# A gated FFN behind windowed attention: a hand-ordered start, a shorter lag between attention and FFN, and another order of loads

## The chip, the cores and the metric

The kernel runs on one core of one Trainium2 chip. The metric is the device time of one execution in microseconds (us); lower is better. A kernel is timed several times, and I quote the median with the lowest and highest run. Runs are sorted into fast and slow (for this one-core kernel a run is slow when it lies over 1.5% above the fastest run of the same kernel). The reported time is about 1.7 us longer than the span of the profile (234.69 against 233.0 us for the profiled run of the kernel before).

## The reference

Eight sequences of 576 positions go through attention with 8 heads of 64. Four heads see a window of 32 positions, four see every fourth position of a window of 128. Then one of eight experts is picked **per sequence**, from the mean over the whole sequence, and applied to all of it.

```python
# attention (cut): scores masked to window 32, or to window 128 with step 4; softmax; attn @ v -> x (8, 576, 512)
pooled = x.mean(axis=1)
logits = pooled @ w_gate
e_idx = np.argmax(logits, axis=1)              # one expert for a whole sequence
...
h = np.maximum(x[mask] @ w1[e], 0.0)           # w1[e]: 512 x 1024
out[mask] = gate_w[mask, None, None] * (h @ w2[e])
```

What matters is a dependence: no weight of a sequence's FFN can be fetched before **all** of its attention is done, because the address of w1 and w2 is the gate's result. In between must be other work, or the TensorE (PE) waits.

## The kernel before

Attention is cut into slots, four to a batch (one slot is two heads). The FFN of batch b runs in four slots too: two for the first matmul (FFN1, with w1), two for the second (FFN2, with w2, and a tail of 64 rows). `LAGS` says how many slots after its attention a batch's FFN runs. Batch 0 has 7, so that the pipeline starts early, the others have 8, so that slot 11 has no FFN work.

```python
LAGS = (7, 8, 8, 8, 8, 8, 8, 8)
...
for b in range(B):
    for kk in range(NSLOT):                        # NSLOT = 4
        runs[NSLOT * b + kk + LAGS[b]] = (b, kk)   # slot t runs quarter kk of the FFN of batch b
...
for t in range(max(runs) + 1):
    ...                                            # items: quarter of an FFN in this slot
    pa(); fence()                                  # first half of attention x V of slot t-1
    flush()                                        # issues the output stores of the last FFN2 slot
    emit_S_mm(b, n); emit_exp(b, n)                # scores of slot t
    run_T(t)                                       # transposes of q or k for a later slot
    ...
    for i, f in enumerate(items[:k0]):             # first half of this slot's FFN work
        f()
        if i == k0 // 2 and gn == 0 and 1 < gb < B + 1:
            emit_gate(gb - 1)                      # gate of batch b: in slot 4b + 5
    ...
    emit_norm(pb, pn)                              # normalise slot t-1; after a batch's last: its mean
    for i, f in enumerate(items[k0:]):             # second half of the FFN work
        f()
```

The gate reads the index into a register of GpSimd (POOL), which then issues the loads. They all go through one software queue (q0 on the page), in this order:

```python
def emit_gate(b):
    ...                                            # four small matmuls, argmax, index to a register
    for a in range(2):
        for g in range(2):                         # w1[e] in four requests, float32 in memory, bf16 in the tile
            nc.gpsimd.dma_start(out=w1b[...], in_=moe_w1[ds(e_val, 1), ...])
    if b == 0:
        load_va(2); load_qb(2)
    load_vb(b + 2)
    nc.gpsimd.dma_start(out=w2b[:], in_=moe_w2[ds(e_val, 1)]...)
    load_qa(b + 3); load_va(b + 3); load_qb(b + 3) # q, k and v, up to three batches ahead
```

Output rows are stored by SyncE (SP) through another queue (q1 on the page). The first seven slots, before any FFN work, were emitted by the same loop in a fixed order.

The softmax here doesn't subtract the row's maximum and nothing guards it: scores larger than these inputs give would overflow.

## Time and profile before

| | before |
|---|---|
| time, median of 3 runs | 232.99 us (232.79 to 236.41) |
| span of the profile | 233.0 us |
| PE busy | 85% |
| mean granted PE clock | 0.967 |
| gate of batch 0, first FFN matmul | 30.15, 41.88 us |
| gate to gate, batches 1 to 7, mean | 24.1 us |

The next lines are from the page of the kernel before: the PE's busy time; then busy tenths of PE, granted PE clock and DMA in 40 slices of the span; then the chain that ended last, by engine and by line.

```profile
PE 199.2 (85%) x3938; PEld 138.9 (60%) x3952; DVE 128.6 (55%) x368; ACT 129.1 (55%) x231; POOL 80.6 (35%) x128
...
PE   0577665999952999999999799999999999999992
...
PEclk9999999999985599999999999999999999999998
DMA  5999319999999947999999999999996299489823
...
PE 74%; DMA 8%; issue 6%; ACT 4%; DVE 4%; POOL 2%; POOLq 1%; SPq 0%
```

After the start the PE is nearly full. The exception is near 66 to 81 us, with the slot that has no FFN work, an idle of 4.5 us that the profile calls "issue" (the engine waited for nothing that the profile shows), and a half clock (granted 0.50 from 67.63 to 81.28). The DMA engines are busy nearly throughout: the packets of the software queue take 90.3% of sixteen engines' span, those of the store queue 12.2%.

How a batch gets its weights in time is seen in one batch. The next lines are from the timeline of PE in the kernel before, batch 3 (start, duration, engine, line, operation, tiles, count). L476 is the gate, L534 is FFN1, L554 and L569 are FFN2 and its tail. (x15 stands where 16 ran: this trace lacks 14 records of L554, x242 in place of x256. A row at the end of a window is cut off there.)

```profile
108.39 0.34 PE L476 MATMUL m<-wg_t,pooled 128*1 128x8 f32 x8
109.24 2.61 PE L534 MATMUL m<-xt,w1b 128*128 128x288 bf16 x20 [0.51 <-DVE mx L481]
...
113.45 3.63 PE L554 MATMUL m<-w2b,ht 128*128 128x512 bf16 x15
...
118.62 3.63 PE L554 MATMUL m<-w2b,ht 128*128 128x512 bf16 x15
122.18 1.06 PE L569 MATMUL m<-w2b,ht 128*64 128x256 bf16 x16
...
124.76 1.52 PE L534 MATMUL m<-xt,w1b 128*128 128x288 bf16 x11
```

And the timelines of POOL and of SP for the same stretch, the first line being w1's requests, the second the first stores of batch 2:

```profile
110.78 2.40 POOL L490 DMA_DIRECT2D w1b<-in_moe_w_dram  x4 [10.39 <-DVE ht L541]
...
117.92 0.81 SPq L562 DMA_DIRECT2D out_dram<-osb  x2
```

The gate runs at 108.39 and w1 is first used at 124.76, that is 16.4 us later, all of it filled: half a slot of FFN1, both slots of FFN2 of the batch before, and attention. The w1 requests go out at 110.78, and the trace has their last landing at 120.78, 4 us before the use.

In the tail there is no attention left to fill with. Batch 7 in the timeline of PE of the kernel before:

```profile
200.53 0.35 PE L476 MATMUL m<-wg_t,pooled 128*1 128x8 f32 x8
...
203.67 7.08 PE L554 MATMUL m<-w2b,ht 128*128 128x512 bf16 x31
210.68 1.06 PE L569 MATMUL m<-w2b,ht 128*64 128x256 bf16 x16
211.68 0.42 PE L534 MATMUL m<-xt,w1b 128*128 128x288 bf16 x2
212.47 7.75 PE L534 MATMUL m<-xt,w1b 128*128 128x288 bf16 x62 [0.37 <-DMA w1b<-in_moe_w_dram]
```

Here w1 and its use just meet: the wait is 0.37 us.

### The profile page before, as it was taken

Reading aid. Unit: us, or ns where it says so; the run is one execution under the profiler, and the core shown is the slowest. Engines: PE = TensorE matmul, PEld = TensorE weight load, DVE = VectorE, ACT = ScalarE, POOL = GpSimd, SP = SyncE. Lnnn points to the kernel's source line nnn. Section 1 sums busy time; section 2 is a strip of 40 time slices with the busy share of each in tenths; the row PEclk is TensorE's granted clock in tenths of the full one; section 3 lists DMA queues with packets and bytes.
Section 4 is the critical chain, followed back from the end, with each engine's and each line's share of the span. In section 5 each row is a group of like instructions: output and inputs, shape, how many; then the busy total and the mean of one; then the engine's idle time right before and its main releaser. Section 6 shows DMA issues by size and latency. Waiting matters only on the chain.

```text
span 233.0 us, 9018 instructions
## 1 busy us (share of the span) xinstructions
PE 199.2 (85%) x3938; PEld 138.9 (60%) x3952; DVE 128.6 (55%) x368; ACT 129.1 (55%) x231; POOL 80.6 (35%) x128
## 2 busy tenths in 40 slices
PE   0577665999952999999999799999999999999992
PEld 0556455775651676587658565777577746746741
DVE  2765464665652465686558466667566657415312
ACT  2466755676552377666865566577657763431420
POOL 7873037640934009520862048405500400130000
PEclk9999999999985599999999999999999999999998
DMA  5999319999999947999999999999996299489823
GB/s 86 180 191 192 72 29 163 190 205 204 178 225 230 204 89 114 160 254 237 207 210 234 239 150 167 205 254 206 199 242 177 44 160 230 137 139 247 177 93 113
DMA packets 49383, 40.97 MB, mean 176 GB/s; under 512 B 23744, under 2 KB 37056, under 8 KB 49344
## 3 DMA queue, kind: packets, MB, share of 16 engines
q0 software_dynamic: 42880, 30.94, 90.3%
q1 hardware_dynamic: 6464, 9.46, 12.2%
q8 instruction: 31, 0.51, 0.8%
q14 instruction: 8, 0.07, 0.1%
HBM read 61.88 MB, written 9.44 MB: 306 GB/s over the span
## 4 chain that ended last, share of the span: by engine, by line
PE 74%; DMA 8%; issue 6%; ACT 4%; DVE 4%; POOL 2%; POOLq 1%; SPq 0%
PE m L534 28%; PE m L554 21%; PE nd L323 8%; DMA w1b<-in_moe_w_dram 6%; PE m L243 5%; PE ps L264 3%; PE m L569 3%; DMA km<-in_k_dram 3%; PE e L323 2%; ACT pt L288 1%; DVE qk L253 1%; ACT qk L251 1%; DVE pt L295 1%; PE m L521 1%; ACT lnd L420 1%
## 5 line engine op out<-in xcount | busy, mean ns | idle before, releaser
L534 PE MATMUL m<-xt,w1b 128*128 128x288 bf16 x512 | 70.5, 296 | 3.0 <-issue 1.6
L534 PEld LDWEIGHTS <-w1b 128*128 128x128 bf16 x512 | 49.9, 101 | 18.8 <-issue 4.1
L554 PE MATMUL m<-w2b,ht 128*128 128x512 bf16 x242 | 56.9, 380 | 1.0 <-issue 0.2
L490 POOL DMA_DIRECT2D w1b<-in_moe_w_dram x32 | 19.1, 612 | 103.5 <-PE m L534 55.9
L539 ACT ACTIVATE ht<-m 128x288 bf16<-128x288 f32 x64 | 26.3, 411 | 30.1 <-PE m L534 26.5
L288 ACT ACTIVATE pt<-ps 128x896 bf16<-128x896 f32 x32 | 29.2, 912 | 23.3 <-PE ps L264 23.3
L554 PEld LDWEIGHTS <-ht 128*128 128x128 bf16 x256 | 23.8, 98 | 27.7 <-DMA w2b<-in_moe_w_dram 0.2
L541 DVE TENSOR_SCALAR ht<-m 128x288 bf16<-128x288 f32 x64 | 28.2, 453 | 13.9 <-PE m L534 13.0
L453 DVE SCALAR_TENSOR_TENSOR xt<-nd,rd 128x320 bf16<-128x320 f32 (+1 forms) x52 | 26.0, 537 | 11.9 <-ACT rd L426 11.9
L253 DVE COPY qk<-m 128x576 bf16<-128x576 bf16 x23 | 17.4, 756 | 22.6 <-PE m L243 22.4
L323 PEld LDWEIGHTS <-vm 64*64 64x64 bf16 x896 | 17.6, 116 | 19.1 <-issue 13.1
L295 DVE TENSOR_TENSOR pt<-pt,mk 128x896 bf16<-128x896 bf16 x32 | 19.8, 620 | 11.5 <-ACT pt L288 11.4
L121 POOL DMA_DIRECT2D vm<-in_v_dram x32 | 24.3, 783 | 5.3 <-DMA qm<-in_q_dram 2.4
L323 PE MATMUL nd<-pt,vm 64*64 64x64 bf16 (+1 forms) x736 | 18.7, 195 | 5.1 <-DMA w1b<-in_moe_w_dram 2.6
L426 ACT ACTIVATE rd<-lnd 128x576 f32<-128x576 f32 x32 | 21.9, 683 | 0.9
L323 PE MATMUL nd<-pt,ones 64*64 64x256 bf16 (+2 forms) x236 | 17.0, 247 | 4.5 <-issue 4.5
L420 ACT ACTIVATE lnd<-nd 128x576 f32<-128x576 f32 x26 | 16.7, 642 | 7.3 <-PE nd L323 7.3
L561 DVE TENSOR_SCALAR osb<-m,gbc 128x512 f32<-128x512 f32 x16 | 12.0, 750 | 15.6 <-PE m L554 15.5
L243 PEld LDWEIGHTS <-km 64*64 64x64 bf16 x576 | 14.7, 123 | 7.9 <-DMA km<-in_k_dram 7.1
L264 PE MATMUL ps<-qk 64*64 64x96 bf16 (+2 forms) x576 | 18.2, 237 | 1.2 <-ACT qk L251 0.8
L264 PEld LDWEIGHTS <-qk 64*64 64x64 bf16 x576 | 16.0, 130 | 1.7 <-issue 1.5
L251 ACT ACTIVATE qk<-m 128x576 bf16<-128x576 bf16 x23 | 16.6, 722 | 0.1
(68 smaller groups left out, 208.0 us busy)
## 6 DMA issues: line engine op xcount, KB each, us to landing
w1b<-in_moe_w_dram POOLq DMA_DIRECT2D x32, 256.0 KB, 6.5
w2b<-in_moe_w_dram POOLq DMA_DIRECT2D x8, 1024.0 KB, 13.9
out_dram<-osb SPq DMA_DIRECT2D x32, 256.0 KB, 6.8
km<-in_k_dram POOLq DMA_DIRECT2D x16, 288.0 KB, 11.6
qm<-in_q_dram POOLq DMA_DIRECT2D x16, 288.0 KB, 12.4
vm<-in_v_dram POOLq DMA_DIRECT2D x8, 256.0 KB, 11.8
vm<-in_v_dram POOLq DMA_DIRECT2D x32, 64.0 KB, 7.3
out_dram<-osx SPq DMA_DIRECT2D x16, 64.0 KB, 7.1
```

What stands on the lines that cost most here:

```text
L121: nc.gpsimd.dma_start(out=t[:, h], in_=v[b, h, 0:512, :].rearrange("(c p) d -> p c d", p=P))
L243: nc.tensor.transpose(out=tp[half(a), j, :], in_=ld[half(a), RH * jh + j, :], identity=ident2[half(a), :])
L264: nc.tensor.matmul(ps[half(e), a, o : o + rhs.free_size()], lhsT=lhsT, rhs=rhs, start=True, stop=True, skip_group_check=True)
L288: nc.scalar.activation(out=pt[:], in_=s["ps"][:, :, 0:NP], func=AF.Exp, scale=0.125)
L295: nc.vector.tensor_tensor(out=pt[:], in0=pt[:], in1=mk[:, g : g + 1, :].to_broadcast([P, 2, NP]), op=ALU.mult)
L323: x = nc.tensor.matmul(oo, lhsT=lhsT, rhs=rhs, start=start, stop=True, skip_group_check=True)
L426: nc.scalar.activation(out=rd[:], in_=s["lnd"][:], func=AF.Exp, scale=-1.0)
L453: nc.vector.scalar_tensor_tensor(out=o, in0=a0, scalar=1.0, in1=a1, op0=ALU.mult, op1=ALU.mult, accum_out=s["pool"][:, w, c : c + 1],)
L534: nc.tensor.matmul(hm, lhsT=s["w1"][:, c, fc * P : (fc + 1) * P], rhs=s["xt"][:, c, cols], start=(c == 0), stop=(c == 3))
L539: nc.scalar.activation(out=o, in_=hm, func=AF.Relu)
L541: nc.vector.tensor_scalar_max(out=o, in0=hm, scalar1=0.0)
L554: nc.tensor.matmul(om, lhsT=s["ht"][:, fc, r * P : (r + 1) * P], rhs=s["w2"][:, fc, :], start=(fc == 0), stop=(fc == 7))
```

## The change

Its intent: reach the first gate and the first FFN matmul sooner, by ordering the first seven slots by hand and by making the masks from fewer operations; let the first FFN matmul start on half of batch 0's w1; run every batch's FFN 7 slots after its attention, so that the slot without FFN goes and the tail is shorter; and put fewer requests ahead of w1 in the queue, by fetching q, k and v later.

```diff
-LAGS = (7, 8, 8, 8, 8, 8, 8, 8)
+LAG = 7
...
-        for a in range(2):
-            for g in range(2):
-                r0 = 256 * g + 128 * a
-                nc.gpsimd.dma_start(... w1, four requests ...)
-        if b == 0:
-            load_va(2)
-            load_qb(2)
+        fs = F // 2 if b == 0 else F
+        for f0 in range(0, F, fs):
+            for a in range(2):
+                for g in range(2):
+                    ... the same four, columns f0 : f0 + fs; eight requests for batch 0
+        load_va(b + 2)
+        load_qb(b + 2)
+        nc.gpsimd.dma_start(out=w2b[:], ...)
         load_vb(b + 2)
-        nc.gpsimd.dma_start(out=w2b[:], ...)
         load_qa(b + 3)
-        load_va(b + 3)
-        load_qb(b + 3)
...
-            runs[NSLOT * b + kk + LAGS[b]] = (b, kk)
+            runs[NSLOT * b + kk + LAG] = (b, kk)
...
+    emit_T(0, a, "k", 0)          # the first seven slots, written out (57 lines, cut); a, z: head groups
+    emit_T(0, a, "q", 1)
+    sl[0].sx()                    # scores and exp of slot 0
+    ...
+    sl[3].norm()
+    emit_gate(0)
+    emit_T(1, a, "q", 1)
+    sl[4].sx()
+    sl[4].mask()
+    emit_T(1, z, "k", 1)
+    sl[4].av_a()
+    sl[5].sx()
+    sl[4].av_b()
+    ...
+    sl[4].norm()
+    emit_T(1, z, "q", 0)          # into the PSUM bank that slot 4's norm reads
+    sl[5].av_a()
+    sl[6].sx()
+    ...
+    for t in range(LAG, NA + LAG):  # from here the loop as before, without a slot that lacks FFN work
+        ...
+        gb, gn = divmod(t - 5, NSLOT)
+        ...
+                emit_gate(gb)     # still in slot 4b + 5
```

The mask part replaces float copies by comparing the integers directly, and the first loads of q, k and v go out in another order (both cut). Note the last lines: the gate stays in slot 4b + 5, but the FFN of its batch moves from slot 4b + 8 to 4b + 7.

More of the change, by code (lines that the diff above doesn't have):

```diff
@@ L151 @@
     make_identity(nc, identb[:])
-    load_v(0, GO[0])
-    load_vt(0)
     dti = const.tile([P, QB], I32, name="dti")
-    nc.gpsimd.iota(dti[:], pattern=[[1, QB]], base=0, channel_multiplier=-1)
+    for a in range(2):
+        nc.gpsimd.iota(dti[64 * a : 64 * a + 64, :], pattern=[[1, QB]], base=0, channel_multiplier=-1)
     dtt = const.tile([P, 4, 16], I32, name="dtt")
@@ L158 @@
     load_qk(0, GO[1])
-    load_v(0, GO[1])
+    load_va(0)
+    load_vb(0)
     load_qa(1)
@@ L183, with masks_a @@
     mk = const.tile([P, 2, NP], BF16, name="mk")
-    def masks():
-        dpf = const.tile([P, QB], F32, name="dpf")
-        nc.vector.tensor_copy(out=dpf[:], in_=dti[:])
-        nc.vector.tensor_scalar(out=dpf[DH:P], in0=dpf[DH:P], scalar1=64.0, scalar2=None, op0=ALU.add)
-        le31 = const.tile([P, QB], F32, name="le31")
-        nc.vector.tensor_scalar(out=le31[:], in0=dpf[:], scalar1=31.0, scalar2=None, op0=ALU.is_le)
+    def masks_a():
         band = const.tile([P, QB], BF16, name="band")
+        le31 = const.tile([P, QB], BF16, name="le31")
+        nc.vector.tensor_scalar(out=le31[:], in0=dti[:], scalar1=31.0, scalar2=None, op0=ALU.is_le)
@@ L192, in masks @@
         nc.vector.scalar_tensor_tensor(
-            out=band[:], in0=dpf[:], scalar=0.0, in1=le31[:], op0=ALU.is_ge, op1=ALU.mult
+            out=band[:], in0=dti[:], scalar=0.0, in1=le31[:], op0=ALU.is_ge, op1=ALU.mult
         )
-        for g in GO:
-            nc.vector.tensor_copy(
-                out=mk[:, g, 0 : 4 * QB].rearrange("p (i n) -> p i n", n=QB),
-                in_=band[:].rearrange("p (i n) -> p i n", i=1).to_broadcast([P, 4, QB]),
-            )
-        nc.vector.tensor_copy(out=mk[:, 0, 4 * QB : NP], in_=band[:, 0:DH])
+        mask_main(1, band)
@@ L201, in masks @@
         dta = const.tile([P, 4, 16], I32, name="dta")
         nc.vector.tensor_scalar(out=dta[:], in0=dtt[:], scalar1=3, scalar2=None, op0=ALU.bitwise_and)
-        dtf = const.tile([P, 4, 16], F32, name="dtf")
-        nc.vector.tensor_copy(out=dtf[:], in_=dta[:])
-        dtg = const.tile([P, 4, 16], F32, name="dtg")
-        nc.vector.tensor_copy(out=dtg[:], in_=dtt[:])
-        nc.vector.tensor_scalar(out=dtg[:], in0=dtg[:], scalar1=0.0, scalar2=None, op0=ALU.is_ge)
+        dtg = const.tile([P, 4, 16], BF16, name="dtg")
@@ L208, in masks, with mask_main @@
+        nc.vector.tensor_scalar(out=dtg[:], in0=dtt[:], scalar1=0.0, scalar2=None, op0=ALU.is_ge)
         nc.vector.scalar_tensor_tensor(
             out=mk[:, 1, 4 * QB : NP].rearrange("p (r m) -> p r m", r=4),
-            in0=dtf[:], scalar=0.0, in1=dtg[:], op0=ALU.is_equal, op1=ALU.mult,
+            in0=dta[:], scalar=0.0, in1=dtg[:], op0=ALU.is_equal, op1=ALU.mult,
         )
+        return band
+    def mask_main(g, band):
+        nc.vector.tensor_copy(
+            out=mk[:, g, 0 : 4 * QB].rearrange("p (i n) -> p i n", n=QB),
+            in_=band[:].rearrange("p (i n) -> p i n", i=1).to_broadcast([P, 4, QB]),
+        )
@@ L213, with masks_b @@
+    def masks_b(band):
+        mask_main(0, band)
+        nc.vector.tensor_copy(out=mk[:, 0, 4 * QB : NP], in_=band[:, 0:DH])
+    band = masks_a()
     st = {}
@@ L226, in half, with emit_T @@
         return slice(64 * a, 64 * a + 64)
-    def emit_T(b, g, nm, t):
+    def emit_T(b, g, nm, t=0):
         s = state(b)
@@ L313, in ndc @@
             return nd[:, o : o + n] if nb is None else nb[o // 512][:, o % 512 : o % 512 + n]
-        s["nd"] = (ndc, lns)
+        s["nd", n] = (ndc, lns)
         first, lasts = [None], []
@@ L413, in av_work, with emit_ln, emit_rd @@
         return part_a, fence, part_b
-    def emit_ln(b):
+    def emit_ln(b, n):
         s = st[b]
         lnd = rdp.tile([P, S], F32, name="lnd", tag="lnd")
-        ndc, lns = s["nd"]
-        for o, n in lns:
-            nc.scalar.activation(out=lnd[:, o - DSO : o - DSO + n], in_=ndc(o, n), func=AF.Ln)
-        s["lnd"] = lnd
-    def emit_rd(b):
+        ndc, lns = s["nd", n]
+        for o, w in lns:
+            nc.scalar.activation(out=lnd[:, o - DSO : o - DSO + w], in_=ndc(o, w), func=AF.Ln)
+        s["lnd", n] = lnd
+    def emit_rd(b, n):
         s = st[b]
         rd = rdp.tile([P, S], F32, name="rd", tag="rd")
-        nc.scalar.activation(out=rd[:], in_=s["lnd"][:], func=AF.Exp, scale=-1.0)
-        s["rd"] = rd
+        nc.scalar.activation(out=rd[:], in_=s["lnd", n][:], func=AF.Exp, scale=-1.0)
+        s["rd", n] = rd
     def emit_norm(b, n):
@@ L432, in emit_norm @@
         c = 2 * g + h2
-        (ndc, _), rd = s["nd"], s["rd"]
+        (ndc, _), rd = s["nd", n], s["rd", n]
         xt = s["xt"][:, c, :]
@@ L486, in emit_gate @@
         s["w1"], s["w2"] = w1b, w2b
-        for a in range(2):
-            for g in range(2):
-                r0 = 256 * g + 128 * a
-                nc.gpsimd.dma_start(
-                    out=w1b[half(a), 2 * g : 2 * g + 2, :],
-                    in_=moe_w1[ds(e_val, 1), r0 : r0 + 128, :].rearrange("e (h d) f -> d (e h) f", d=DH),
-                )
-        if b == 0:
-            load_va(2)
-            load_qb(2)
+        fs = F // 2 if b == 0 else F
+        for f0 in range(0, F, fs):
+            for a in range(2):
+                for g in range(2):
+                    r0 = 256 * g + 128 * a
+                    nc.gpsimd.dma_start(
+                        out=w1b[half(a), 2 * g : 2 * g + 2, f0 : f0 + fs],
+                        in_=moe_w1[ds(e_val, 1), r0 : r0 + 128, f0 : f0 + fs].rearrange("e (h d) f -> d (e h) f", d=DH),
+                    )
+        load_va(b + 2)
+        load_qb(b + 2)
+        nc.gpsimd.dma_start(out=w2b[:], in_=moe_w2[ds(e_val, 1)].rearrange("e (c p) f -> p (e c) f", p=P))
         load_vb(b + 2)
-        nc.gpsimd.dma_start(out=w2b[:], in_=moe_w2[ds(e_val, 1)].rearrange("e (c p) f -> p (e c) f", p=P))
         load_qa(b + 3)
-        load_va(b + 3)
-        load_qb(b + 3)
     def emit_gate_w(b):
@@ L601 @@
         for kk in range(NSLOT):
-            runs[NSLOT * b + kk + LAGS[b]] = (b, kk)
-    run_T(-2)
-    run_T(-1)
-    masks()
-    for t in range(max(runs) + 1):
-        if t == LAGS[0]:
-            late()
-        b, n = divmod(t, NSLOT)
-        pb, pn = divmod(t - 1, NSLOT)
-        fb, fk = runs.get(t, (-1, 0))
-        att = t < NA
-        prev = 0 <= t - 1 < NA
-        items = []
-        if fb >= 0:
-            if fk < 2:
-                for x in range(8):
-                    items.append(lambda x=x: ffn1(fb, 4 * fk + x // 2, x % 2, "D" if x < 4 else "A"))
-            elif fk == 2:
-                items += [lambda: ffn2(fb, 0, "A"), lambda: ffn2(fb, 1, "D")]
-            else:
-                items += [lambda: ffn2(fb, 2, "A"), lambda: ffn2(fb, 3, "D"), lambda: ffn_tail(fb)]
-        early_on = pools["early"] is not None
-        if early_on:
-            if att and n % 2:
-                emit_S_mm(b, n)
-                emit_exp(b, n)
-            if prev:
-                pa, fence, pbb = av_work(pb, pn)
+            runs[NSLOT * b + kk + LAG] = (b, kk)
@@ L631, with __init__, sx, mask @@
+    class slot:
+        def __init__(self, t):
+            self.b, self.n = divmod(t, NSLOT)
+            self.on = 0 <= t < NA
+        def sx(self):
+            if self.on:
+                emit_S_mm(self.b, self.n)
+                emit_exp(self.b, self.n)
+        def mask(self):
+            if self.on:
+                emit_mask(self.b, self.n)
+        def av_a(self):
+            if self.on:
+                pa, fence, self.pb = av_work(self.b, self.n)
                 pa()
                 fence()
-                pbb()
@@ L634, with av_b @@
-            if att and n % 2 == 0:
-                if prev:
-                    emit_ln(pb)
-                emit_S_mm(b, n)
-                emit_exp(b, n)
-            elif prev:
-                emit_ln(pb)
-            if prev:
-                emit_rd(pb)
-            emit_mask(b, n)
-            run_T(t)
-        else:
-            if prev:
-                pa, fence, pbb = av_work(pb, pn)
-                pa()
-                fence()
-            flush()
-            if att:
-                emit_S_mm(b, n)
-                emit_exp(b, n)
-            if items:
-                run_T(t)
-            if prev:
-                if not att and items:
-                    items.pop(0)()
-                pbb()
-                emit_ln(pb)
-            if att:
-                emit_mask(b, n)
-            if prev:
-                emit_rd(pb)
-            if not items:
-                run_T(t)
+        def av_b(self):
+            if self.on:
+                self.pb()
@@ new lines, in ln, with rd, norm @@
+        def ln(self):
+            if self.on:
+                emit_ln(self.b, self.n)
+        def rd(self):
+            if self.on:
+                emit_rd(self.b, self.n)
+        def norm(self):
+            if self.on:
+                emit_norm(self.b, self.n)
+                if self.n == NSLOT - 1:
+                    emit_pooled(self.b)
+    sl = [slot(t) for t in range(NA + LAG + 1)]
+    a, z = GO
+    emit_T(0, a, "k", 0)
+    emit_T(0, a, "q", 1)
+    sl[0].sx()
+    emit_T(0, z, "k", 0)
@@ new lines @@
+    sl[0].mask()
+    sl[1].sx()
+    sl[0].av_a()
+    sl[0].av_b()
+    sl[0].ln()
+    emit_T(0, z, "q", 1)
+    sl[1].mask()
+    masks_b(band)
+    sl[0].rd()
+    sl[1].av_a()
+    sl[2].sx()
+    sl[1].av_b()
+    sl[0].norm()
+    sl[1].ln()
+    sl[1].rd()
+    sl[2].mask()
+    sl[2].av_a()
+    sl[3].sx()
+    sl[2].av_b()
+    sl[1].norm()
+    sl[2].ln()
+    sl[2].rd()
+    sl[3].mask()
+    sl[3].av_a()
+    sl[2].norm()
+    sl[3].av_b()
+    emit_T(1, a, "k", 0)
+    sl[3].ln()
@@ new lines @@
+    sl[3].rd()
+    sl[3].norm()
[7 more added lines that the diff above has]
+    sl[4].av_b()
+    sl[4].ln()
+    sl[4].rd()
+    sl[5].mask()
+    sl[4].norm()
+    emit_T(1, z, "q", 0)
+    sl[5].av_a()
+    sl[6].sx()
+    sl[5].av_b()
+    sl[5].ln()
+    sl[5].rd()
+    sl[6].mask()
+    sl[5].norm()
+    emit_gate_w(0)
+    late()
+    tsched[LAG] = [(2, a, "k")]
+    for t in range(LAG, NA + LAG):
+        cur, pre = sl[t], sl[t - 1]
+        fb, fk = runs[t]
+        if fk < 2:
+            items = [
+                lambda x=x: ffn1(fb, 4 * fk + x // 2, x % 2, "D" if x < 4 else "A") for x in range(8)
+            ]
+        elif fk == 2:
+            items = [lambda: ffn2(fb, 0, "A"), lambda: ffn2(fb, 1, "D")]
+        else:
+            items = [lambda: ffn2(fb, 2, "A"), lambda: ffn2(fb, 3, "D"), lambda: ffn_tail(fb)]
+        pre.av_a()
+        flush()
+        cur.sx()
+        run_T(t)
+        if pre.on and not cur.on:
+            items.pop(0)()
+        pre.av_b()
+        pre.ln()
+        cur.mask()
+        pre.rd()
@@ L667 @@
         k0 = len(items) // 2
-        gb, gn = divmod(t - 1, NSLOT)
+        gb, gn = divmod(t - 5, NSLOT)
         for i, f in enumerate(items[:k0]):
             f()
-            if i == k0 // 2 and gn == 0 and 1 < gb < B + 1:
-                emit_gate(gb - 1)
-        if not items[:k0] and gn == 0 and 1 < gb < B + 1:
-            emit_gate(gb - 1)
-        if prev:
-            emit_norm(pb, pn)
-        if prev and pn == NSLOT - 1:
-            emit_pooled(pb)
+            if i == k0 // 2 and gn == 0 and 0 < gb < B:
+                emit_gate(gb)
@@ L679 @@
+        pre.norm()
         for i, f in enumerate(items[k0:]):
             f()
-        if t == NSLOT:
-            emit_gate(0)
-        if gn == 1 and 0 < gb < B + 1:
-            emit_gate_w(gb - 1)
-        if fb >= 0 and fk == 1:
+            if t == LAG and i == 0:
+                emit_T(2, a, "q")
+        if gn == 1 and 0 < gb < B:
+            emit_gate_w(gb)
+        if fk == 1:
             emit_gate_bc(fb)
```

## The prediction

> **What bounds the kernel now.** The page gives a span of 233.0 us, with PE busy 85% and the chain of waits 74% on PE. The software DMA queue's packets take 90% of sixteen engines' span. Each batch hangs on its gate (timeline and DMA issues): the gate matmul of batch 7 starts at 200.53, the first w1 issue follows at 202.90, the last w1 quarter lands at 212.33 and w2 at 220.64, where FFN2 starts at once. First w1 issue to last w1 landing took 9.2 to 10.9 us, so gate to usable w1 is about 11.6 us. Lag 8 hides that: for batch 2 the gate is at 85.57 and w1 is first used at 101.21, 15.6 us later.
>
> **The first slots.** The gate falls at 30.15, the first FFN matmul at 41.87, when w1 has just landed. Chaining traced durations (exp 0.92, mask 0.63, AV 1.3, log 0.7, reciprocal 0.68, norm 0.85 to 1.2, copies 0.73) along the new engine orders, I put the gate at about 27.4: fewer transposes precede it and km of group 0 lands about 2 us earlier. But slots 4 to 6 become a serial loop (norm of slot 4, then the last transposes of batch 1 in the same bank, then scores of slot 6, its exp, log, norm), so the first FFN matmul comes near 44.5, although the w1 column half lands near 36. On the old order the same arithmetic is 1 us late. Mask operations (2.9 us of VectorE before) were on the chain for only about 1 us.
>
> **Lag 7 gains** the slot without FFN (64.4 to 68.5, with PE idle 2.3 us), and perhaps the 4.5 us "issue" idle at 71 and the half clock that follows (granted 0.50 from 67.8 to 81.2). [...]
>
> **Lag 7 costs.** From gate to first use only 9.6 us of PE work remain (timeline, 90 to 101: one FFN2 block 1.75, the slot with the tail 6.1, attention 1.6). Against 11.6 us that is about 2 us of idle PE per batch for batches 2 to 6. w2 now lies behind va and qb (about 4.5 us of queue instead of 1.6): I expect it about 12.5 us after w1, where PE needs it after 11.6. So the period from gate to gate becomes 25 to 26 us against 23.3 mean. In the tail the gate of batch 7 comes after the first FFN2 block of batch 6; only 6.3 us of work cover the 11.6, so 5 us idle, and w2 again sets the end, 32.5 us after that gate.
>
> **Sum (estimate).** Gate of batch 1 near 59.5 (56 before), five periods of 25, 23 to gate 7, 32: 240 us. A half clock after the longer idles could add a few us.
>
> Predicted 240 us, range 231 to 249; faster by over 2%: 0.13, within 2%: 0.2, slower: 0.67.
>
> **What would show it.** Right: gate at 27 to 28; first FFN near 44; PE idle 1.5 to 3 us on DMA w1 before each batch's first FFN matmul, 4 us or more before batch 7. Wrong: first FFN before 40, no w1 waits.
>
> **What would make it wrong.** w1 landing within 7 us of its first issue; slots 4 to 6 running faster than chained; the issue idle and half clock being worth more than lag 7 costs.

The sum is 59.5 + 5 × 25 + 23 + 32 = 239.5 us, given as 240; the half clock was left to the margin, as the author's estimate.

## The result, and the profile after

The changed kernel takes **265.33 us** (264.31 to 266.29, 4 fast runs), the kernel before 233.56 us (232.79 to 236.41, 4 runs). The ratio is 1.137, with a 95% interval of 1.129 to 1.146: **slower by 14%**. (A ratio here is the mean time of one kernel's fast runs over that of the other's in the same rounds, so not quite the ratio of the medians. Below, "ratio" always means a kernel's time over that of the kernel before.) The direction was as predicted; the time lies 16 us above the top of the range.

The page after:

```profile
PE 209.0 (79%) x3952; PEld 141.8 (54%) x3952; DVE 129.2 (49%) x364; ACT 129.0 (49%) x231; POOL 83.1 (31%) x133
...
PE   1663646999699958998599939997699949955993
...
PEclk9999999999979997999689997999599988996899
DMA  6999299904999599949999599939991796199213
...
PE 48%; DMA 32%; issue 9%; POOL 3%; DVE 3%; POOLq 2%; ACT 1%; SPq 0%
```

The PE row now has a dip at a regular distance, and after each dip the clock row has one too: seven stretches of 3.41 or 6.83 us at a granted clock of 0.50, one in each of batches 1 to 7. The chain that ended last was 74% PE and is now 48% PE and 32% DMA. The list of waits of PE in the changed kernel begins so (total us, times, longest us); the kernel before has no wait of FFN1 for w1 among its first nine lines:

```profile
PE m L534 <- DMA w1b<-in_moe_w_dram: 28.5, 14, 4.2
```

Batch 4 in the timeline of PE after (L477 is the gate now):

```profile
144.81 0.34 PE L477 MATMUL m<-wg_t,pooled 128*1 128x8 f32 x8
145.09 1.90 PE L554 MATMUL m<-w2b,ht 128*128 128x512 bf16 x8
...
148.33 3.63 PE L554 MATMUL m<-w2b,ht 128*128 128x512 bf16 x16
151.88 1.06 PE L569 MATMUL m<-w2b,ht 128*64 128x256 bf16 x16
...
157.42 0.42 PE L534 MATMUL m<-xt,w1b 128*128 128x288 bf16 x2 [3.11 <-DMA w1b<-in_moe_w_dram]
159.10 5.21 PE L534 MATMUL m<-xt,w1b 128*128 128x288 bf16 x30 [1.26 <-DMA w1b<-in_moe_w_dram]
```

And in the timelines of POOL (w1's requests) and SP (the stores of batch 3) after:

```profile
147.12 1.80 POOL L493 DMA_DIRECT2D w1b<-in_moe_w_dram  x3 [12.71 <-PE m L554]
149.91 0.60 POOL L493 DMA_DIRECT2D w1b<-in_moe_w_dram  x1 [1.00 <-issue]
...
147.60 6.73 SPq L562 DMA_DIRECT2D out_dram<-osb  x4
154.44 1.99 SPq L581 DMA_DIRECT2D out_dram<-osx  x2
```

From gate to first use there is now one slot and a half of FFN2 with its attention, and PE has run out of work at 154.3. The four w1 quarters land at 151.70, 154.47, 157.38 and 159.05, so PE waits twice, for the third and for the fourth. And **all six stores of the batch before are issued between the w1 requests and w1's landing**. In the kernel before the load of batch 4 had none.

After the wait the clock is halved: the trace has it at 0.50 from 158.51 to 161.92. These are windows of FFN1 of the same batch (window, its length, PE busy with the count, weight loads, then the granted clock, DMA share, GB/s; the share can pass 1, because a packet is counted whole where it starts):

```profile
159.10:162.50 3.40, 3.40 (x17) 2.24 (x18) 0.58 1.29 225
...
165.90:169.90 4.00, 4.00 (x32) 2.97 (x32) 1.00 1.67 188
```

17 matmuls in 3.4 us at a clock of 0.58, against 32 in 4.0 us at full clock.

The tail, batch 7 after:

```profile
228.51 0.34 PE L477 MATMUL m<-wg_t,pooled 128*1 128x8 f32 x8
228.78 5.35 PE L554 MATMUL m<-w2b,ht 128*128 128x512 bf16 x24
234.07 1.06 PE L569 MATMUL m<-w2b,ht 128*64 128x256 bf16 x16
239.38 0.42 PE L534 MATMUL m<-xt,w1b 128*128 128x288 bf16 x2 [4.25 <-DMA w1b<-in_moe_w_dram]
241.46 10.58 PE L534 MATMUL m<-xt,w1b 128*128 128x288 bf16 x62 [1.65 <-DMA w1b<-in_moe_w_dram]
```

The wait is 4.25 and 1.65 us in place of 0.37, and the same 62 matmuls take 10.58 us in place of 7.75, again on a lower clock (0.73 on average over them, 1.00 before). From gate 7 to the end it is 36.1 us.

Where the prediction's sum went wrong is seen from the gates and landings in both traces. "Load" is first w1 issue to last w1 landing; "stored" is what the store queue moved during it; "rest" is the time that the 30 matmuls take which FFN1's first slot still has after the last wait.

| batch | before: load us | stored KB | after: load us | stored KB | after: gate to w1 landed | after: w1 landed to next gate | after: rest us |
|---|---|---|---|---|---|---|---|
| 1 | 10.91 | 612 | 10.07 | 534 | 12.36 | 14.90 | 5.51 |
| 2 | 9.40 | 0 | 11.64 | 886 | 13.88 | 14.67 | 5.27 |
| 3 | 10.00 | 85 | 11.06 | 719 | 13.37 | 15.97 | 6.58 |
| 4 | 9.77 | 0 | 11.94 | 948 | 14.24 | 14.52 | 5.21 |
| 5 | 9.94 | 61 | 11.43 | 796 | 13.74 | 15.72 | 6.42 |
| 6 | 9.16 | 0 | 10.61 | 699 | 12.91 | 12.57 | 5.51 |
| 7 | 9.43 | 170 | 10.53 | 845 | 12.81 | (end) | |

### The profile page after: what moved, and what is told of

Read it like the earlier page. It is cut to its first block, busy times and chain, and to the rows that moved or that the text cites. A ratio compares the mean times of both kernels' runs of the same rounds, so it can differ in the third digit from the quotient of the medians.

```text
span 264.6 us, 9030 instructions
## 1 busy us (share of the span) xinstructions
PE 209.0 (79%) x3952; PEld 141.8 (54%) x3952; DVE 129.2 (49%) x364; ACT 129.0 (49%) x231; POOL 83.1 (31%) x133
## 4 chain that ended last, share of the span: by engine, by line
PE 48%; DMA 32%; issue 9%; POOL 3%; DVE 3%; POOLq 2%; ACT 1%; SPq 0%
PE m L534 29%; DMA w1b<-in_moe_w_dram 24%; PE m L554 7%; PE nd L324 4%; PE m L244 3%; DMA vm<-in_v_dram 3%; DMA qm<-in_q_dram 3%; DMA km<-in_k_dram 2%; PE ps L265 2%; POOLq L484 2%; PE m L521 1%; POOL w1b L493 1%; PE m L477 1%; POOLq L493 1%; DVE mi L482 1%
## 5 line engine op out<-in xcount | busy, mean ns | idle before, releaser
L534 PE MATMUL m<-xt,w1b 128*128 128x288 bf16 x512 | 81.9, 326 | 28.7 <-DMA w1b<-in_moe_w_dram 28.5
L534 PEld LDWEIGHTS <-w1b 128*128 128x128 bf16 x512 | 54.9, 111 | 52.3 <-issue 17.7
L554 PE MATMUL m<-w2b,ht 128*128 128x512 bf16 x256 | 58.9, 380 | 0.0
L493 POOL DMA_DIRECT2D w1b<-in_moe_w_dram x36 | 21.5, 614 | 109.9 <-PE m L554 71.6
L539 ACT ACTIVATE ht<-m 128x288 bf16<-128x288 f32 x64 | 26.3, 411 | 59.5 <-PE m L534 56.3
L554 PEld LDWEIGHTS <-ht 128*128 128x128 bf16 x256 | 23.3, 98 | 26.4
L254 DVE COPY qk<-m 128x576 bf16<-128x576 bf16 x24 | 18.1, 755 | 21.7 <-PE m L244 21.0
L324 PEld LDWEIGHTS <-vm 64*64 64x64 bf16 x896 | 16.8, 115 | 15.6 <-issue 5.3
L324 PE MATMUL nd<-pt,vm 64*64 64x64 bf16 (+1 forms) x736 | 18.0, 194 | 3.3 <-DMA km<-in_k_dram 3.3
L265 PE MATMUL ps<-qk 64*64 64x96 bf16 (+2 forms) x576 | 17.6, 237 | 2.0 <-ACT qk L252 1.9
L561 DVE TENSOR_SCALAR osb<-m,gbc 128x512 f32<-128x512 f32 x16 | 12.0, 751 | 12.7 <-PE m L554 12.0
L252 ACT ACTIVATE qk<-m 128x576 bf16<-128x576 bf16 x24 | 17.3, 721 | 0.3 <-PE m L244 0.3
L244 PEld LDWEIGHTS <-km 64*64 64x64 bf16 x576 | 14.0, 122 | 5.8 <-DMA km<-in_k_dram 5.8
## 6 DMA issues: line engine op xcount, KB each, us to landing
vm<-in_v_dram POOLq DMA_DIRECT2D x8, 256.0 KB, 11.5
vm<-in_v_dram POOLq DMA_DIRECT2D x32, 64.0 KB, 11.6
```

What stands on the lines that cost most here:

```text
L244: nc.tensor.transpose(out=tp[half(a), j, :], in_=ld[half(a), RH * jh + j, :], identity=ident2[half(a), :])
L265: nc.tensor.matmul(ps[half(e), a, o : o + rhs.free_size()], lhsT=lhsT, rhs=rhs, start=True, stop=True, skip_group_check=True)
L324: x = nc.tensor.matmul(oo, lhsT=lhsT, rhs=rhs, start=start, stop=True, skip_group_check=True)
L493: nc.gpsimd.dma_start(out=w1b[half(a), 2 * g : 2 * g + 2, f0 : f0 + fs], in_=moe_w1[ds(e_val, 1), r0 : r0 + 128, f0 : f0 + fs].rearrange(" ...
L534: nc.tensor.matmul(hm, lhsT=s["w1"][:, c, fc * P : (fc + 1) * P], rhs=s["xt"][:, c, cols], start=(c == 0), stop=(c == 3))
L539: nc.scalar.activation(out=o, in_=hm, func=AF.Relu)
```

## The experiments

My theory after seeing this: lag 7 is the whole loss, in three layers. (1) The gate stays where it was while its use moves a slot nearer, so the w1 load no longer fits under the work left. This was predicted. (2) The same move brings the output stores into the w1 load, and it grows by some 2 us. (3) Each wait then costs a half clock. Rivals: the new first slots or the new load order are what costs; the load is slow for another reason than the stores; the clock matters little.

Fifteen kernels were run. Two missed what was expected of them in a way that taught something: a_lag8 and b_late. The first was cleared up by a further run, the second was not. (a_late_stores and a_lag8_old came out 0.5 and 1.3 us below their ranges.)

| kernel | edit | us, median (range) | ratio (95%) |
|---|---|---|---|
| after | | 265.33 (264.31 to 266.29) | 1.137 (1.129 to 1.146) |
| b_lag7 | before + lag 7 | 262.44 (260.68 to 267.93) | 1.122 (1.115 to 1.128) |
| a_lag8 | after + lag 8 | 243.37 (241.92 to 245.1) | 1.043 (1.036 to 1.050) |
| a_lag8_old | after + lag 8 + old loads | 232.69 (231.64 to 236.55) | 0.997 (0.987 to 1.007) |
| a_old_loads | after + old loads | 263.47 (262.06 to 267.38) | 1.127 (1.120 to 1.133) |
| a_front | after + another order of the start | 261.83 (257.01 to 265.18) | 1.105 (1.086 to 1.124) |
| a_whole_w1 | after + w1 of batch 0 whole | 263.91 (262.39 to 268.59) | 1.130 (1.119 to 1.141) |
| a_old_masks | after + old masks | 267.12 (265.16 to 267.71) | 1.147 (1.139 to 1.155) |
| a_late_stores | after + later stores | 247.48 (247.18 to 253.28) | 1.057 (1.050 to 1.065) |
| a_fill | after + dummy matmuls in the wait | 256.00 (255.35 to 256.16) | 1.095 (1.089 to 1.100) |
| a_gate_early | after + gate most of a slot sooner | 236.59 (233.5 to 237.49) | 1.011 (1.002 to 1.020) |
| b_lag7_gate | before + lag 7 + early gate | 234.15 (233.99 to 235.51) | 1.007 (1.002 to 1.012) |
| b_lag7_gate_late | the same + later stores | 229.03 (228.82 to 229.67) | 0.983 (0.979 to 0.987) |
| b_late | before + later stores | 231.18 (227.81 to 233.18) | 0.977 (0.965 to 0.989) |
| n1 | after + another start + early gate + later stores | **227.31 (226.82 to 228.36)** | **0.972 (0.965 to 0.978)** |
| n2 | n1 with old loads | 230.71 (229.73 to 231.58) | 0.987 (0.980 to 0.993) |

Medians and ranges hold all runs, the ratios only fast ones. In the rounds that held a_front, n1, n2, b_late, a_lag8_old, a_whole_w1 and a_old_masks the kernel before had two or three slow runs of seven, and the record calls each of these verdicts "unclear" at its 2% threshold, as it does for b_lag7_gate_late; for them I go by the interval alone. The profiled runs of b_lag7, a_front, a_whole_w1, a_gate_early and b_late fell in the slow state; for those I rely on the times, and use the profile only for when a load was issued and landed or for the order of work.

### Which part of the change costs: lag, loads, start, masks

**b_lag7**: the kernel before with nothing but the lag.

```diff
-LAGS = (7, 8, 8, 8, 8, 8, 8, 8)
+LAGS = (7, 7, 7, 7, 7, 7, 7, 7)
```

> The kernel before with lag 7 for every batch, nothing else changed. Theory: it takes over most of the loss although it has the old start and the old load order: PE waits for w1 of 2 to 4 us before each batch from 2 on, half clock after them, 255 to 265 us. Rival (lag 7 alone is harmless, the loss needs the new load order): at most 238 us.

It took 262.44 us: lag 7 alone makes 12 of the 14 per cent. The first slots and the loads are not needed for the loss.

**a_lag8**: the changed kernel with the old lags.

```diff
-            runs[NSLOT * b + kk + LAG] = (b, kk)
+            runs[NSLOT * b + kk + LAGS[b]] = (b, kk)      # (7, 8, 8, 8, 8, 8, 8, 8); slot 11 without items
```

> The changed kernel with lag 8 given back to batches 1 to 7 and nothing else undone (hand-ordered first slots, new masks, w1 halves, new load order all kept). Theory (lag 7 leaves too little work between a gate and the first use of its w1): no waits of the PE on w1 before batches 2 to 6, periods from gate to gate of 23 to 24.5 us, and a time of 231 to 239 us, the first FFN matmul staying near 44.5 us. Rival (the new load order or the hand-ordered start carries the loss): 255 us or more.

It took 243.37 us, 22 us less than the changed kernel, but 4 us above what I expected, and 4% above the kernel before. The waits for w1 are gone. A new one is there, in the timeline of PE of a_lag8:

```profile
78.80 1.06 PE L245 MATMUL m<-ident,km 64*64 64x64 bf16 x32 [5.12 <-DMA km<-in_k_dram]
```

The km tile of batch 3's second head group had been requested at 66.11, behind w1 of batch 1, and landed at 78.75. In the old order it goes out with batch 0's gate. A half clock of 10.2 us begins at 74.15. That this made up the miss was only argued until the next run.

**a_lag8_old**: lag 8 as above, and the old order and depth of loads.

```diff
-        load_va(b + 2)
-        load_qb(b + 2)
+        if b == 0:
+            load_va(2)
+            load_qb(2)
+        load_vb(b + 2)
         nc.gpsimd.dma_start(out=w2b[:], ...)
-        load_vb(b + 2)
         load_qa(b + 3)
+        load_va(b + 3)
+        load_qb(b + 3)
```

> The changed kernel with lag 8 and the old load order and depth. Theory: the run with lag 8 alone was slow because km of batch 3 landed at 78.75 behind w1, for a PE gap of 5.12 us at 73.68 and a half clock of 10.2 us after it; with the old order km is there by about 65, the gap is gone, and the time falls from 243.4 to 234 to 239 (the later first FFN, 44.2 against 41.9, stays, and perhaps the 4.5 us 'issue' idle of the kernel before near 70 comes back). Rival: the new first slots are what costs; then the time stays at 241 or more with the gap gone.

It took 232.69 us, slightly below the expected range: the km wait is gone, and so is the rest of the miss. At lag 8 the new load order costs about 10.7 us (243.37 against 232.69). What remains of the change here, the hand-ordered start with its masks and halves, gives nothing: ratio 0.997 (0.987 to 1.007).

**a_old_loads**: the load edit alone, at lag 7.

> The changed kernel with the order and depth of loads of the kernel before (vb, w2, then q, k, v of the batch after next but one), all else kept. Theory: at most gates the queue is empty when w1 is issued, so that fewer requests ahead help w1 only at the first gates, and the stores stay: within 2% of the changed kernel, 260 to 269 us, w1 issue to landing still above 10.5 us. Rival (the new order puts stores and w1 on each other): 255 us or less.

It took 263.47 us, within 1% of the changed kernel. So "w1 behind fewer requests" is worth nothing at lag 7, where w1 is issued into a nearly empty queue anyway (in batches 1 to 7 of the changed kernel at most 0.06 us of older requests were ahead of it), and is a loss at lag 8. (With early gates it becomes a gain: see n2.)

**a_whole_w1** and **a_old_masks**: the two small parts undone.

```diff
-        fs = F // 2 if b == 0 else F
+        fs = F                                   # a_whole_w1
```

> The changed kernel with batch 0's w1 in whole rows again, four requests in place of eight. Theory: the first FFN matmul waits for the serial slots before it (44.5), not for w1, which lands near 39 either way; no change, 262 to 268, first FFN 44.2 to 44.8. Rival: the halves bring the first FFN forward; then it comes at 45.5 or later here and the time rises by 1 us or more.

```diff
-        nc.vector.tensor_scalar(out=le31[:], in0=dti[:], ...)          # a_old_masks
+        nc.vector.tensor_copy(out=dpf[:], in_=dti[:])                  # integers to float first
+        nc.vector.tensor_scalar(out=dpf[DH:P], in0=dpf[DH:P], scalar1=64.0, ...)
+        nc.vector.tensor_scalar(out=le31[:], in0=dpf[:], ...)
...                                               # the same for the dilated part; all masks ahead of slot 0
```

> The changed kernel with the old mask operations, all of them ahead of the first qk copy. Theory: VectorE is idle for 1.5 us before that copy (6.56) and the masks are first read at 11.5, so the extra operations are hidden or delay the first copy by under 1 us; gate within 27.0 to 28.0, time within 1% of the changed kernel, 262 to 268. Rival: the masks are on the chain; then the gate moves by 1 us or more.

263.91 and 267.12 us: neither differs from the changed kernel beyond the scatter of the runs. With whole rows the first FFN matmul came at 44.77 (slow profile), with the old masks at 44.34 and the gate at 27.00; the changed kernel has 44.51 and 27.20. Neither part was on the chain.

**a_front**: another hand order of slots 0 to 6. Batch 1's four transposes go between the attention of slots 2 to 4, so that slot 4's norm no longer holds up a transpose.

```diff
     sl[2].ln()
+    sl[3].mask()
+    emit_T(1, a, "k", 1)
...
     sl[3].ln()
-    sl[3].rd()
-    sl[3].norm()
-    emit_gate(0)
-    emit_T(1, a, "q", 1)
+    emit_T(1, a, "q", 0)
+    sl[3].rd()
+    sl[3].norm()
+    emit_T(1, z, "q", 0)
     sl[4].sx()
     sl[4].mask()
     emit_T(1, z, "k", 1)
+    emit_gate(0)
...
-    sl[4].norm()
-    emit_T(1, z, "q", 0)
     sl[5].av_a()
```

> The changed kernel with another order of the work around the first gate: the four transposes of batch 1 are put between slots 2 and 4, into banks that are free there, in place of after the norms (so no transposes wait for the norm of slot 4). All else as changed. Theory (the serial loop norm 4, transposes, scores 6 is what made the first FFN matmul late): first gate within 1 us of 27.2, first FFN matmul from 44.5 to between 37 and 40 us, when the first half of w1 has landed, time down by 4 to 7 us to about 259 us, since the rest is bound by the chain of gates. Rival (the start is bound by DMA or ACT as a whole): first FFN matmul at 43 us or later, time within 1%.

The first FFN matmul came at 39.13, 5.4 us sooner than in the changed kernel and 2.75 us sooner than before (the gate falls at 29.29). The two fast runs took 257.01 and 260.43 us, about 4 to 9 us less than the changed kernel's 264.31 to 266.29 and in line with the 4 to 7 expected; the median of all four, 261.83, contains two slow runs. In the profile, which is one of the slow runs, gate 1 was 4.4 us earlier (55.24 against 59.66) and gate 7 only 2.0 us (226.48 against 228.51); whether a fast run gives part of the better start back in this way is not shown.

### What lag 7 is made of: stores, clock, gate

**a_late_stores**: the stores wait until FFN1's second slot, when w1 is in; the last batch is left as it was.

```diff
         pre.av_a()
-        flush()
+        if fk == 1 or fb == B - 1:
+            flush()
```

> The changed kernel with the output stores of a batch issued one to two slots later, in the slot after the next batch's w1 has landed (the last batch as before). Theory (stores that now fall into the 10 us of a w1 load slow it): first w1 issue to last w1 landing back from 10.6 to 11.9 us to about 9.4, waits on w1 shorter by 1.5 to 2.5 us per batch, time 248 to 256 us. Rival (w1 is slower for another reason, the clock or the order of the queue): issue to landing stays above 10.5 us, time 262 us or more.

It took 247.48 us, 18 us less, just below the range that was expected. Loads of w1 took 8.74 to 9.71 us in batches 1 to 6, and 11.17 in batch 7, whose stores had not been moved. The periods from gate to gate were 24.75, 24.92, 26.21, 24.63, 25.20 and 23.60: what the prediction had. Batch 4 in the timeline of PE and in a window of FFN1 of a_late_stores:

```profile
136.05 0.35 PE L477 MATMUL m<-wg_t,pooled 128*1 128x8 f32 x8
...
146.36 0.42 PE L534 MATMUL m<-xt,w1b 128*128 128x288 bf16 x2 [0.80 <-DMA w1b<-in_moe_w_dram]
147.58 3.85 PE L534 MATMUL m<-xt,w1b 128*128 128x288 bf16 x30 [0.80 <-DMA w1b<-in_moe_w_dram]
```

```profile
147.58:151.43 3.85, 3.85 (x30) 2.85 (x30) 1.00 1.29 207
```

The waits are 0.80 and 0.80 us in place of 3.11 and 1.26, and FFN1 runs on at full clock. From 44.51 to 180 us of this run the granted clock was 1.00, from 180 to 240 it was 0.91. So the stores are the second layer, and shortening the waits took most of the third along.

**a_fill**: the waits stay, but PE is given dummy matmuls into a bank that FFN1 overwrites.

```diff
         hm = bank()[:, 0:HALF]
+        if fc == 0 and hf == 0 and b > 0:
+            for _ in range(FILL[b]):                # (0, 20, 32, 32, 32, 32, 32, 48)
+                nc.tensor.matmul(hm, lhsT=s["xt"][:, 0, 0:P], rhs=s["xt"][:, 0, cols], start=True, stop=True)
```

> The changed kernel with idle-time matmuls put in just before the first FFN matmul of batches 1 to 7 (20, then 32 each, 48 for batch 7; the result is overwritten), so that the PE stays busy while it waits for w1. They shorten no DMA. Theory (a second cost, the half clock after each wait, is worth about 10 us over batches 1 to 6 and 2.8 in batch 7): granted clock 1.00 throughout, first FFN half slot back from 5.2 to 6.6 us to about 4 us, time 250 to 256 us. Rival (the half clock is hidden behind the DMA chain): 262 us or more.

It took 256.00 us, 9.3 us less than the changed kernel, with **more** work on PE. The loads still took 10.25 to 11.52 us. The window of FFN1's first slot in batch 4 of a_fill:

```profile
154.55:158.40 3.85, 3.85 (x32) 2.85 (x30) 1.00 1.26 241
```

In every batch here the last 30 matmuls of FFN1's first slot take 3.83 to 3.85 us, the "rest" of the table above. The mean granted clock of its runs was 0.995 to 1.000, where the changed kernel has 0.934 to 0.935. So the half clock was worth about 9 us by itself.

**a_gate_early**: the gate moves from slot 4b + 5 to the second half of slot 4b + 4, right after the mean is known.

```diff
         for i, f in enumerate(items[:k0]):
             f()
-            if i == k0 // 2 and gn == 0 and 0 < gb < B:
-                emit_gate(gb)
...
         for i, f in enumerate(items[k0:]):
             f()
+            if i == 1 and gn == 3 and 0 < gb + 1 < B:
+                emit_gate(gb + 1)
```

> The changed kernel with the gates of batches 1 to 7 emitted about 5.5 us earlier (in the slot in which the pooled sum becomes ready, two FFN1 items after it, instead of after the first FFN2 block of the slot behind), lag 7 kept. Theory (what lag 7 lacks is distance between gate and first w1 use): distance up from 9.6 to about 15 us, no PE wait on w1 before batches 2 to 6, at most 3 us before batch 7, hardly any half clock, 228 to 238 us. Rival (the DMA queue as a whole is the limit and only moves its waits): 250 us or more.

It took 236.59 us, 29 us less: nearly the whole loss. Waits for w1 are left only before batch 7. Lag 7 is not bad in itself; lag 7 with the gate where it was is. (The gate comes some 4.6 us of work sooner: in batch 4 of this kernel 14.1 us lie between the gate and the first use, where the changed kernel had 9.5 us of work.) One thing moves along: with the gate earlier, most of the stores leave the w1 load too (at most 201 KB stored in batches 1 to 6, loads of 8.71 to 10.18 us). So this run removes the first and the second layer together. What the short distance costs without the stores is seen in a_late_stores, which still takes 247.48 us. By estimate from the table above, 14.1 us would nearly cover even the 12.4 to 14.2 us from gate to w1 with stores beside it.

**b_lag7_gate** and **b_lag7_gate_late**: the kernel before with lag 7 and the early gate (the same edit), then with the later stores too.

> The kernel before with lag 7 for every batch and the gates moved 5.5 us earlier (its own start, masks, loads and whole w1). If distance is all that lag 7 lacks, this keeps the gain that lag 7 was meant for (no slot without FFN, 4 us, and the half clock there): 222 to 231 us. If the old load depth holds w1 up behind its queue, PE waits on w1 of 1 us and more remain and it takes 232 to 242 us.

> The kernel of b_lag7_gate with output stores held back until the next batch's second FFN1 slot, as in a_late_stores. If stores still fall into a w1 load that matters: faster than b_lag7_gate by 2 us or more. If w1 now lands well ahead of its use, the stores' place is indifferent: within 1%.

234.15 us, the second branch of what was expected: the early w1 of batch 1 stood behind 7.7 us of older requests and took 13.55 us. With the later stores 229.03 us, 5 us less, so that stores matter here too, but hardly through w1: PE's waits for w1 fell from 3.0 to 1.2 us, while its idles called "issue" after 45 us fell from 6.5 to 2.0 us (on these see "Not settled" below).

**b_late**: the kernel before, lag 8, with the later stores only.

```diff
-            flush()
+            if fk in (-1, 1) or fb == B - 1:
+                flush()
```

> The kernel before (lag 8) with the stores held back as in a_late_stores. With lag 8 the gate falls in the second FFN1 slot, so that here the hold moves the stores into the w1 load instead of out of it. Theory (stores slow a w1 load, and that costs time only where the distance from gate to use is short): w1 issue to landing up from 9.2 to 10.0 us to 10.5 to 12 us for batches 2 to 6, time within 1.5% of before because 15 us of work lie between. Rival (stores don't matter to w1): landing stays at 9.2 to 10.0.

This missed. I expected loads up to 12 us and a level time; the loads took 9.2 to 10.1 us and the time fell to 231.18 us (the two fast runs 227.81 and 229.86; ratio 0.977, interval 0.965 to 0.989). In batch 3, 992 KB were stored during a load that took only 10.08 us; but there 2.4 us of older requests still stood ahead of w1. It limits the store theory, as follows.

**How much the stores cost.** I took every w1 load of batches 1 to 7 in all the profiles (one landing was not readable). Of 118 loads, 74 were issued with less than 0.5 us of older requests ahead. For those a straight line fits: time = 8.9 us + 2.8 us per MB stored meanwhile, correlation 0.94. The 15 with under 150 KB stored took 9.07 us on average (8.56 to 9.43) for w1's 1 MB tile of four 256 KB requests, the 50 with over 500 KB took 11.01 us (9.92 to 12.23): no overlap. Without the profiles in the slow state it is 48 loads, 8.9 us and 2.7 us per MB. Over all 118 the correlation is only 0.68: where older requests stood ahead, some loads with 0.5 to 1.0 MB of stores took only 9.2 to 10.1 us (in b_late, b_lag7_gate_late and n1), others 10.9 to 11.8 us (batch 1 of the kernel before, batch 2 of a_old_loads). Why the first escape is open.

The stores did not stand behind w1. In batch 4 of the changed kernel they were issued from 147.60 on, after w1's first request at 147.12, and 948 KB of them moved before w1 had landed at 159.05. With 534 to 948 KB of stores beside them the loads of that kernel took 10.07 to 11.94 us, 1.0 to 2.9 us more than the 9.07 us above. How the two queues divide the DMA engines between them was not shown.

### A version that beats both

**n1**: the changed kernel with the order of a_front, the early gate and the later stores.

> A version meant to beat both: the changed kernel with the order of a_front, the early gates of a_gate_early and the late stores of a_late_stores. If the three act where the earlier runs showed: first FFN matmul at 37 to 40 us, no waits on w1 over 1 us before batches 1 to 6, 222 to 228 us. If the new load order brings q, k late now that everything runs ahead: PE waits on km or qm of 1 us and more, 229 us or more.

227.31 us, ratio 0.972 (0.965 to 0.978). Its runs, 226.82 to 228.36, lie below every fast run of the kernel before in the same rounds (233.16 to 234.76). But most of this gain may be the later stores: b_late, the kernel before with nothing else, has 0.977 (0.965 to 0.989) in the same rounds, and no run shows what the early gate and the start add to it at lag 8. Batch 4 in the timeline of PE of n1:

```profile
123.25 0.35 PE L477 MATMUL m<-wg_t,pooled 128*1 128x8 f32 x8 [0.52 <-DVE pooled L469]
...
126.49 3.63 PE L554 MATMUL m<-w2b,ht 128*128 128x512 bf16 x16
...
131.42 3.63 PE L554 MATMUL m<-w2b,ht 128*128 128x512 bf16 x16
134.98 1.06 PE L569 MATMUL m<-w2b,ht 128*64 128x256 bf16 x16
...
137.34 4.37 PE L534 MATMUL m<-xt,w1b 128*128 128x288 bf16 x32
```

Gate to first use is 14.1 us, with both FFN2 slots in between, and no wait. Over the whole run w1 is waited for twice, 2.1 us in all, and the mean granted clock is 0.999.

**n2**: n1 with the old loads.

> As n1 but with the order and depth of loads of the kernel before. Against n1 it tells what 'w1 behind fewer requests' is worth once gates are early: if deep prefetch only delays w1 of batch 1 (landing 11.6 to 13.6 us after issue instead of 9), slower than n1 by 0 to 3 us; if late q and k are the larger cost, faster than n1.

230.71 us. Here w1 of batches 1 and 2 takes 13.81 and 11.60 us behind older requests (9.18 and 9.16 in n1). With early gates the new load order is worth about 1.5%, the same part that cost 10.7 us at lag 8.

## Why the prediction was right or wrong

**Right: the start.** Gate at 27.20 (predicted 27.4), first FFN matmul at 44.51 (44.5), gate 1 at 59.66 (59.5). The serial loop of slots 4 to 6 is in the list of waits as predicted, as a wait of 2.7 us of a transpose for the norm of slot 4. a_whole_w1 bears out that w1's halves were off the chain. The 1 us that the prediction gave to the masks is not seen: with the old masks the gate came at 27.00, no later than with the new ones.

**Right: the direction and the mechanism of lag 7.** b_lag7 shows that lag 7 alone is slower by 12%, and a_gate_early that the gate's distance to its use, with the stores that fall into it, is the reason. Only 9.6 us of work between gate and use was right (batch 4: 144.81 to 154.3).

**Wrong: the size of the period, "25 to 26 us".** The periods are 27.26, 28.55, 29.34, 28.76, 29.46 and 25.48, in sum 168.9 in place of 148 (five of 25 and one of 23). (The prediction's 23.3 us for the kernel before is not found in its trace either: gates 1 to 7 are 24.1 us apart on average, gates 2 to 7 23.0.) Two terms were mis-sized.

- "**gate to usable w1 is about 11.6 us**" was read from the low end of the kernel before (11.5 to 13.2 us in batches 1 to 7, in most of them with next to no stores beside the load) and carried over unchanged. It was 12.4 to 14.2 us, in sum 10.9 us more over batches 1 to 6; 3.8 us of these were there already in the kernel before. `flush()` in the loop showed that stores follow the FFN2 slots, and lag 7 puts these slots under the load. a_late_stores takes the stores away and gets the predicted 25 us.
- "**A half clock after the longer idles could add a few us**" named the mechanism and left it out of the sum. FFN1's first slot took 5.2 to 6.6 us after its last wait where it takes 3.83 us at full clock, in every batch: 11.5 us in sum over batches 1 to 6, and 2.8 us more in batch 7. a_fill shows 9.3 us for it by itself. The two terms don't add cleanly, for shorter waits also spare the clock: a_late_stores alone gives 18 us.

The remaining 36.1 us after gate 7 against 32.5 are 1.2 us of load and 2.8 us of clock, less 0.4 us elsewhere. The path was another one, too: the prediction let w2 set the end, but w2 landed at 247.08 and FFN2 began only at 252.27, so that w1 and the slow FFN1 set it.

**Wrong, without effect: w2.** I expected w2 to land after it was needed. In batch 2 it landed at 111.82, FFN2 began at 113.64; in no batch did PE wait for it. Counted from w1's landing, w2 came 7.7 to 12.7 us later in batches 1 to 6 (predicted 12.5), and FFN2 began 10.7 to 14.1 us later (predicted 11.6), with FFN1 partly at half clock before it.

**Missed: the load order at lag 8.** The prediction saw the new order only as bringing w2 later. It also brings km of batch b + 2 behind w1, which at lag 8 costs 10.7 us (a_lag8 against a_lag8_old) and at lag 7 hides behind the wait for w1 (265.33 us, and 263.47 with the old loads).

**Not settled: lag 7's gain.** The prediction allowed for the slot without FFN (2.3 us idle), and perhaps for the 4.5 us "issue" idle and the half clock at 68 us. The 4.5 us idle is gone in the changed kernel and in b_lag7 (0.6 us there), but also in a_lag8_old, which has lag 8; b_late still has 3.4 us of it at the same place. So it can't be booked to the lag. The traces give a hint of what it is. Over all 17 kernels PE has 33 idles called "issue" of at least 0.4 us after 45 us, and each ends 1.2 to 1.7 us after the end of a 16 KB packet on the queue that the page lists as "q8 instruction"; PE's other idles of that length end 0 to 14 us after one. Before the 4.5 us idle such packets started at 63.2 and then only at 72.9. That PE's instructions came late is the author's guess from this; it was not shown, and no run tests it.

**Not settled: how little idling halves the clock.** In batch 1 of the changed kernel idles of 1.60 and 0.98 us with two FFN1 matmuls between them, about 3 us in all, came before 3.41 us of half clock (from 73.18). Idles of 0.80 and 0.80 us (a_late_stores, batch 4) and a lone 1.65 us between FFN1 matmuls in the kernel before (at 128.4) left the clock at 1.00.

## What to carry to other kernels

When a pipeline is shortened by a stage, ask what else moves with it: here the store flushes came to lie on the critical load, which a load time read from the old profile cannot show. The waits of a few us on the matmul engine had a second price in its clock, 1.4 to 2.8 us a batch here, so it belongs into the sum and not into the margin. If a load hangs on a computed index, move the computation of the index first; with the gate less than a slot earlier the same lag went from 14% slower to 1% slower, and with later stores and another order of the start to 3% faster. But look at the cheap parts one by one: later stores alone took the kernel before to a ratio of 0.977.
